# Loading x behind the casting transfers: 180 loads moved from the sync engine's queue to GpSimd's

## The chip, the cores and the metric

The kernel runs on one core of one Trainium2 chip. Its engines work side by side, each through its own list of instructions in order: TensorE (PE, with its weight loads shown apart as PEld), VectorE (DVE), ScalarE (ACT), GpSimd (POOL) and SyncE (SP). Transfers between DRAM and the on-chip memory are issued by SP, ACT or POOL and carried by 16 DMA engines that all of them share. The metric is device time in microseconds from launch to end.

## The reference

Two layers stand one behind the other. The first is an attention through 32 learned rows ("inducing"), for 4 batches of 12480 rows of 128 numbers; the second is a feed-forward layer with a squared ReLU.

```python
B, N, m, C = (4, 12480, 32, 128)
def mab(q, kv):
    s = scale * (q @ kv.transpose(0, 2, 1))
    s = s - s.max(-1, keepdims=True)
    a = np.exp(s)
    a /= a.sum(-1, keepdims=True) + 1e-09
    return a @ kv
h = mab(I, x)                  # 32 rows look at all of x
attn_out = mab(x, h)           # each row of x looks at those 32
hid = np.maximum(attn_out @ w_in, 0.0)      # 128 -> 2048
out = hid * hid @ w_out                     # 2048 -> 128
```

So x is read twice: all of a batch is needed to make h, and then every row again to be looked up in h. All data is float32.

## The kernel before, in words

A batch is cut into 13 units of 960 rows, so that there are 52 units. For each unit there is a *first* pass (scores of x against the 32 learned rows, a running softmax, a running sum h) and later a *second* pass (scores of x against h, softmax, then the feed-forward layer on the result). The first passes of batch 0 are done alone at the start. After that the kernel does the second passes one unit after another, and puts the first passes of the next batch between them: 39 units in all, units 0 to 12 of batches 1 to 3.

**The loads that the change touches.** Each of these 39 first passes needs x in two forms. `xn` is the unit as it lies, one DMA of 120 partitions by 8 rows of 128 numbers (line 418): 960 runs of 512 bytes. `xq` is the unit in blocks, four DMAs of 32 partitions by 30 groups of 32 numbers (line 438): 960 runs of 128 bytes each. DVE turns `xq` into `xt` in one instruction (line 444). There are three `xn` buffers and one `xq` buffer. PE scores `xt` (line 477) and later adds up `xn` under the weights (line 528).

**The feed-forward layer.** A unit is done in two halves of 480 rows, each in four quads j of four 128-wide slices of the hidden layer. For a quad, PE makes the hidden slices (line 895, output h), ACT applies ReLU (line 903) and squares (line 913) into g. To multiply in two parts of lower precision, g is rounded to `hi` and DVE subtracts to get `lo` (line 924). Then PE adds 12 products to the output op (line 940): hi by wo_hi, hi by wo_lo, lo by wo_hi. In quads 0 and 2 DVE does the rounding (line 920). In quads 1 and 3 a DMA on POOL's queue does it, since that queue's transfers can change the type on the way (line 918). These are the *casting transfers*: four per unit, 200 in all, each 128 partitions by 1920 numbers. There are five g, three hi and two lo buffers, counted over all quads.

**Queues.** Before the change SP's queue carries all loads of x, all stores of the output (line 960, four per half unit), and the way of the second pass's weights through DRAM and back (lines 781 and 797). POOL's queue carries, from the first unit's end on, only the casting transfers.

**What sets the order.** The program hands a planner a list of tasks, with an engine, an assumed duration, a due time, the tasks that must come before, and the buffers taken. The planner walks through time with these assumptions and puts each engine's tasks in an order; the instructions are then written in that order, and on the chip each engine goes through its list and waits where it must. POOL's queue is the planner's engine "CAST". So a task moved from one queue to another also changes the order of everything else.

Of the kernel before, what the change touches and what calls it, by code (L numbers as in the profile page):

```python
# [44 lines left out]
class Plan:  # L45
# [36 lines left out]
    def run(self):  # L82
        free = {e: 0.0 for e in self.ENGINES}
        mode = None
        port = moving = 0.0
        taken = {}
        open_ = {e: [] for e in self.ENGINES}
        done = []

        def offer(t):  # L90
            t.ready = 0.0
            for n in t.needs:
                own = n.by in ("PE", "SP") and t.engine == [n.by]
                t.ready = max(t.ready, n.end if own else n.done + self.LATENCY[n.by] + t.late)
            for e in t.engine:
                open_[e].append(t)

        for t in self.tasks:
            t.waiting = len(set(t.needs))
            for n in set(t.needs):  # L100
                n.then.append(t)
        for t in self.tasks:
            if not t.waiting:
                offer(t)

        def room_at(t):
            at = 0.0
            n = {}
            for b in t.takes:
                n[b.tag] = n.get(b.tag, 0) + 1  # L110
                old = taken.get(b.tag, [])
                if b.turn is not None and b.turn != len(old):
                    return None
                i = len(old) + n[b.tag] - 1 - self.room[b.tag]
                if i >= 0:
                    for u in (old[i].users if i < len(old) else ()):
                        if u.end is None:
                            return None
                        at = max(at, u.done + 100.0 + t.late)
            return at  # L120

        while len(done) < len(self.tasks):
            best = None
            for e in self.ENGINES:
                pick = None
                for t in open_[e]:
                    at = room_at(t) if t.takes else 0.0
                    if at is None:
                        continue
                    start = max(free[e], t.ready, at)  # L130
                    if e == "POOL" or (e == "DVE" and t.port):
                        start = max(start, port)
                    key = (0.0 if start <= free[e] + t.near else start, t.due, t.order)
                    if pick is None or key < pick[0]:
                        pick = (key, start, t)
                if pick and (best is None or (pick[1], pick[2].due) < best[0]):
                    best = ((pick[1], pick[2].due), pick[1], pick[2], e)
            if best is None:
                raise RuntimeError("the plan is stuck")
            _, start, t, e = best  # L140
            for k in t.engine:
                open_[k].remove(t)
            ns = t.ns[t.engine.index(e)] if isinstance(t.ns, tuple) else t.ns
            if e == "PE":
                if t.mode != mode:
                    start += self.SWITCH
                mode = t.mode
            t.by, t.start, t.end = e, start, start + ns
            t.done = t.end
            if t.moves:  # L150
                moving = max(moving, t.end + self.FIRST) + t.moves
                t.done = moving + self.LAST + t.lag
            free[e] = t.end
            if e == "POOL" or (e == "DVE" and t.port):
                port = t.end
            for b in t.takes:
                taken.setdefault(b.tag, []).append(b)
            done.append(t)
            for n in t.then:
                n.waiting -= 1  # L160
                if not n.waiting:
                    offer(n)
        return done
# [3 lines left out]
def induced_attention_then_squared_relu_ffn(  # L167
# [8 lines left out]
    nc = tc.nc  # L176
    B, N, C = x.shape
# [4 lines left out]
    NU = N // UNIT  # L182
# [7 lines left out]
    PERIOD, START, T_MAIN, NARROW, STEP = 31000.0, 2500.0, 56000.0, -6000.0, 1300.0  # L190
    W_LOAD = [3000.0, 10500.0, 25400.0, 29700.0, 31000.0, 32000.0, 33000.0, 34000.0]
    W_DUE = [12000.0, 19500.0, 36000.0, 38000.0, 40000.0, 44000.0, 48000.0, 52000.0]
    W_SUM = [50000.0, 54000.0, 57000.0, 60000.0]
    WIDE_NS, STRIPS, AWAY = 870, -34000.0, 0.0
    NEAR, REST_LAG = 450.0, 6000.0
    LAG, CAST_LAG, TWICE, WITHOUT = 1500.0, 1500.0, (3, 6, 9, 14, 27), (12, 25)
# [22 lines left out]
    x_v = x.rearrange("b (u j p) c -> b u p j c", j=NT, p=TS)  # L219
# [31 lines left out]
    add = plan.add  # L251
# [148 lines left out]


    class First:
        def __init__(self, b, u, due, early=False, behind=None, after=None):

            self.b, self.u, self.early, self.n = b, u, early, f"{b}_{u}"
            self.s = s = state.setdefault(b, {"xt": {}, "chain": None, "bxt": {}})
            self.bx = Buffer("early" if early else "xn")
            self.bt = s["bxt"][u] = Buffer("xt")
            lead = 2500 if early else 8000

            def load():
                self.xn = (pools["early"] if early else xn_pool).tile(
                    [TS, NT, C], F32, tag="xn", name=f"xn_{self.n}"
                )
                if early:
                    nc.sync.dma_start(self.xn.rearrange("p (k j) c -> p k (j c)", k=2), xe_v[b, u])
                else:
                    nc.sync.dma_start(self.xn, x_v[b, u])

            loaded = add(  # L420
                "SP", 450, load, due - lead - (4000 if early else 12000), [after],
                takes=[self.bx], late=0, moves=1950 if early else 2300, lag=0.0 if early else LAG,
            )
            self.turned = []
            if not early:
                self.turned.append(self.turn_blocks(due - lead, behind, after))
                return
            for k in range(2):
                self.turned.append(self.turn(k, due - lead + k * lead * 0.4, loaded))

        def turn_blocks(self, due, behind, after):
            bq = Buffer("xq")
            v = {}

            def load():
                v["xq"] = xq_pool.tile([P, 1024], F32, tag="xq", name=f"xq_{self.n}")
                for q in range(Q):
                    nc.sync.dma_start(
                        v["xq"][q * M:(q + 1) * M, :UNIT].rearrange("p (g c) -> p g c", c=M), xq_v[self.b, self.u, q]
                    )  # L440

            def turned():
                self.xt = self.s["xt"][self.u] = xt_pool.tile([C, UNIT], F32, tag="xt", name=f"xt_{self.n}")
                nc.vector.transpose(self.xt, v["xq"][:, :UNIT])  # L444

            t = add("SP", 2200, load, due - 16000, [after], takes=[bq], late=0, moves=3200, lag=LAG)
            return add("DVE", 1070, turned, due, [t, behind], takes=[self.bt], reads=[bq])

        def turn(self, k, due, loaded):
# [423 lines left out]
    def ffn_block(b, u, k, second, t0, opened):  # L873
        n = f"{b}_{u}_{k}"
        s = state[b]
        w = {}
# [3 lines left out]
        sums, done = [], []  # L880

        def quad(j):
# [39 lines left out]
            def low():  # L922
# [1 line left out]
                nc.vector.tensor_sub(v["lo"], v["g"], v["hi"])  # L924

            sq = add("ACT", 1706, square, due + 4000, relus, reads=[bg], late=0)
            cast = j % 2 and 2 < 2 * (b * NU + u) + k < 2 * B * NU - 1
            th = add("CAST" if cast else "DVE", 550 if cast else 1070, high, due + 5700, [sq] + (opened[1:] if j else []), port=not cast,
                     late=200, takes=[bhi], reads=[bg], moves=2800.0 * cast, lag=CAST_LAG * cast)
            tl = add("DVE", 2070, low, due + 7800, [th] + (opened[1:] if j else []), port=True, late=0, takes=[blo], reads=[bg, bhi])  # L930
            for m, (wo, name, from_, buf) in enumerate((
                (wo_hi, "hi", th, bhi), (wo_lo, "hi", th, bhi), (wo_hi, "lo", tl, blo),
# [39 lines left out]

    units = [(b, u) for b in range(B) for u in range(NU)]
    w_ins, w_outs = load_weights(W_DUE)
    firsts = {}
    for u in range(NU):
        firsts[u] = First(0, u, 6000 + START * u, early=True)
        first_alone(firsts[u], 6000 + START * u)
# [15 lines left out]
    open_stage()  # L994
    done = NU - 1

    def next_first(due, after):
        nonlocal done
        if done + 1 == len(units):
            return None  # L1000
        done += 1
        firsts[done] = First(*units[done], due, after=after)
        return firsts[done]

    for w, (b, u) in enumerate(units):
# [10 lines left out]
            seconds[w + 1] = Second(*nxt)  # L1016
        for m in range(1 + (w in TWICE)):
            g = firsts[done] if state.get("last") is not firsts[done] else None
            f = None if w in WITHOUT else next_first(t_u + NARROW, seconds[0].ready[1])
            narrow(None if m or not w else seconds[w + 1], f, g, t_u + NARROW, STEP, before)  # L1020
    for t in plan.run():
        t.fn()
# [31 lines left out]
```

## Time and profile before

| what | value |
|---|---|
| median of 3 runs | 1621.87 us (1618.33 to 1624.77) |
| the profiled execution's own time | 1619.65 us |
| its span, first to last instruction | 1617.9 us |
| granted TensorE clock, mean | 0.997 |
| busy PE, PEld, DVE, ACT, POOL | 99%, 82%, 89%, 95%, 7% |

The span is what the profile shows instruction by instruction; the profiled execution's own time is 1.75 us longer. A busy share is the time in which an engine's instructions ran, waits left out. Matmuls are pipelined, so their records overlap and a busy PE still has to be read through what it waited for. In lists of groups, `out<-in` gives the tiles by the program's names, and what stands behind the bar is the group's busy time, the mean duration of one instruction, the idle time of the engine just before them, and what ended most of that idle time.

### The profile page before, as it was taken

The numbers are of one execution on the slowest core, as the hardware profiler recorded it, in microseconds if no ns is written. First come the engines' busy times: TensorE is split into PE (matmuls) and PEld (weight loads), VectorE is DVE, ScalarE is ACT, GpSimd is POOL, SyncE is SP. The second block draws the span as 40 slices with busy tenths as digits, with TensorE's granted clock in tenths as the row PEclk, the third lists the DMA queues.
The fourth block names the chain that finished last, engine by engine and source line by source line (L and its number), as shares of the span: only waits on it lengthen the run. The fifth ranks groups of instructions, "written<-read, shape, count | busy, mean of one in ns | idle before, by whom it ended". The sixth has DMA issues, their size and how long they took to land.

```text
span 1617.9 us, 23615 instructions
## 1 busy us (share of the span) xinstructions
PE 1594.3 (99%) x8713; PEld 1322.2 (82%) x8713; DVE 1435.6 (89%) x1577; ACT 1541.3 (95%) x1566; POOL 114.8 (7%) x213
## 2 busy tenths in 40 slices
PE   7899999999999999999999999999999999999998
PEld 5488888888888888888888888888888888888886
DVE  4799899988999989998999889989888888989897
ACT  6799999999999999999999999999999999999995
POOL 0000000000000000000000000000000000000000
PEclk9999999999999999999999999999999999999999
DMA  9559889976997797886898898766557555665653
GB/s 225 116 102 225 223 215 217 219 213 182 229 248 201 197 215 205 214 205 189 214 222 232 201 207 207 200 191 177 177 176 222 181 178 178 186 174 183 197 166 89
DMA packets 476735, 315.48 MB, mean 195 GB/s; under 512 B 365996, under 2 KB 445084, under 8 KB 476620
## 3 DMA queue, kind: packets, MB, share of 16 engines
q1 hardware_dynamic: 446508, 116.96, 40.2%
q0 software_dynamic: 29024, 196.84, 34.9%
q8 instruction: 68, 1.11, 0.3%
q14 instruction: 47, 0.39, 0.1%
q10 hardware_dynamic: 1088, 0.18, 0.1%
HBM read 77.15 MB, written 39.67 MB: 72 GB/s over the span
## 4 chain that ended last, share of the span: by engine, by line
PE 90%; DMA 3%; ACT 3%; DVE 2%; issue 1%; SPq 0%; ACTq 0%; DVEq 0%; POOLq 0%
PE op L940 63%; PE h L895 22%; PE na L726 2%; ACT g L903 2%; DMA hi<-g 1%; PE na L477 1%; DMA words_i<-in_moe_w_in_dram 1%; PE nb L528 1%; ACT g L913 1%; DVE lo L924 1%; PE ep L508 1%; DMA xn<-in_x_dram 0%; DMA words_o<-in_moe_w_out_dram 0%; DVE hi L920 0%; PE xtp L459 0%
## 5 line engine op out<-in xcount | busy, mean ns | idle before, releaser
L924 DVE TENSOR_TENSOR lo<-g,hi 128x1920 fp32r<-128x1920 f32 x416 | 882.2, 2144 | 36.0 <-PE op L940 20.7
L903 ACT ACTIVATE g<-h 128x960 f32<-128x960 f32 x832 | 777.8, 983 | 30.3 <-PE h L895 27.6
L913 ACT ACTIVATE g<-g 128x1920 f32<-128x1920 f32 x416 | 759.3, 1825 | 4.3
L895 PE MATMUL h<-st,hw 128*128 128x480 f32 x1664 | 503.4, 385 | 3.5 <-ACT g L903 2.5
L940 PE MATMUL op<-hi,wo_lo 128*128 128x480 f32 x1664 | 475.4, 379 | 0.0
L940 PE MATMUL op<-lo,wo_hi 128*128 128x480 f32 x1664 | 435.2, 381 | 1.3 <-DVE lo L924 1.3
L940 PE MATMUL op<-hi,wo_hi 128*128 128x480 f32 x1664 | 433.1, 380 | 1.8 <-DMA hi<-g 1.8
L895 PEld LDWEIGHTS h<-st,hw 128*128 128x128 f32 x1664 | 304.4, 188 | 64.3 <-ACT g L903 10.1
L940 PEld LDWEIGHTS op<-hi,wo_hi 128*128 128x128 f32 x1664 | 310.9, 188 | 52.5 <-DMA hi<-g 2.8
L940 PEld LDWEIGHTS op<-lo,wo_hi 128*128 128x128 f32 x1664 | 309.5, 188 | 52.4 <-DVE lo L924 2.8
L940 PEld LDWEIGHTS op<-hi,wo_lo 128*128 128x128 f32 x1664 | 311.4, 188 | 50.0 <-issue 1.2
L920 DVE CAST hi<-g 128x1920 fp32r<-128x1920 f32 x216 | 247.6, 1148 | 22.3 <-PE op L940 13.6
L918 POOL DMA_DIRECT2D hi<-g x200 | 110.4, 552 | 1417.5 <-PE op L940 374.9
L956 DVE STREAM_TRANSPOSE rows<-op 128x480 f32<-128x480 f32 x104 | 70.7, 680 | 57.6 <-PE op L940 56.4
L444 DVE STREAM_TRANSPOSE xt<-xq 128x960 f32<-128x960 f32 x39 | 45.4, 1165 | 3.4 <-DMA xq<-in_x_dram 1.9
L726 PEld LDWEIGHTS na<-xt,hT 128*32 128x32 f32 x520 | 19.9, 110 | 24.4 <-issue 17.9
L726 PE MATMUL na<-xt,hT 128*32 128x256 f32 (+2 forms) x520 | 34.8, 351 | 0.4 <-ACT hT L255 0.4
L754 DVE TENSOR_REDUCE z<-d 128x8 f32<-128x256 f32 x52 | 20.7, 398 | 12.7 <-ACT d L750 12.6
L740 DVE STREAM_TRANSPOSE d<-na 128x256 f32<-128x256 f32 x52 | 23.0, 442 | 6.9 <-PE na L726 6.9
L528 PE MATMUL nb<-xn,et 120*32 120x128 f32 x624 | 25.7, 276 | 0.0
L477 PE MATMUL na<-xt,indT 128*32 128x240 f32 x312 | 24.3, 368 | 0.0
L255 ACT COPY xt<-xtp 128x480 f32<-128x480 f32 x26 | 14.2, 559 | 10.6 <-PE xtp L459 10.6
(95 smaller groups left out, 508.0 us busy)
## 6 DMA issues: line engine op xcount, KB each, us to landing
hi<-g POOLq DMA_DIRECT2D x200, 960.0 KB, 4.9
xn<-in_x_dram SPq DMA_DIRECT2D x52, 480.0 KB, 6.4
out_dram<-rows SPq DMA_DIRECT2D x414, 60.0 KB, 3.4
st<-far SPq DMA_DIRECT2D x102, 240.0 KB, 4.6
xq<-in_x_dram SPq DMA_DIRECT2D x156, 120.0 KB, 5.5
far<-sw SPq DMA_DIRECT2D x51, 240.0 KB, 2.5
hw<-hwfar SPq DMA_DIRECT2D x24, 128.0 KB, 4.4
words_i<-in_moe_w_in_dram SPq DMA_DIRECT2D x4, 512.0 KB, 14.9
```

Of the source, the lines that this page charges most:

```text
L444: nc.vector.transpose(self.xt, v["xq"][:, :UNIT])
L477: nc.tensor.matmul(to, indT, from_, start=True, stop=True)
L528: nc.tensor.matmul(where[q * M:(q + 1) * M, :], self.et[:, k, q * M:(q + 1) * M], self.xn[:, 2 * q + k, :], start=(k == 0), stop=(k == 1),)
L726: nc.tensor.matmul(where[q * M:(q + 1) * M, to:to + n], self.s["hT"][:, :2 * M].rearrange("c (m a) -> c m a", a=2)[:, :, 0], self.s["xt"][ ...
L895: nc.tensor.matmul(c["hp"][:, l, :BLK], s["hw", j][:, f % 4 * P:(f % 4 + 1) * P], s["st", u][:, k, :], start=True, stop=True,)
L903: nc.scalar.activation(v["g"][:, 2 * i:2 * i + 2, :], c["hp"][:, :, :BLK], AF.Relu)
L913: nc.scalar.activation(v["g"], v["g"], AF.Square)
L918: nc.gpsimd.dma_start(v["hi"], v["g"])
L920: nc.vector.tensor_copy(v["hi"], v["g"])
L924: nc.vector.tensor_sub(v["lo"], v["g"], v["hi"])
L940: nc.tensor.matmul(w["op"][:, :BLK], wo[:, 4 * j + l, :], v[name][:, l, :], start=len(done) == 1, stop=len(done) == 3 * NF,)
L956: nc.vector.transpose(w["rows"].rearrange("p g c -> p (g c)"), w["op"][:, :BLK])
```

## The change

The loads of x for units 3 and later leave SP's queue and are issued by POOL, each placed behind one chosen casting transfer. `CASTS` says which: for a unit's turn w in the loop, `xq` behind the second half's quad 1 of the unit two before, `xn` behind the same quad of the unit one before; where two first passes fall in one turn, the second pair goes behind other quads. Only units 0 to 2 of batch 1 stay on SP, because no casting transfer is there for them yet; the other 36 of the 39 move. "Behind" is an order in one queue and no wait for the cast to land: `own` makes the planner take the cast's issue, not its landing, as the point from which the load may go. `XN_NS` and 2400 are the planner's assumed issue times.

```diff
-                own = n.by in ("PE", "SP") and t.engine == [n.by]
+                own = n.by in ("PE", "SP", "CAST") and t.engine == [n.by]
...
+    CASTS, XN_NS = (((-2, 1, 1), (-1, 1, 1)), ((-1, 0, 1), (-1, 1, 3))), 900
...
-                    nc.sync.dma_start(self.xn, x_v[b, u])
+                    (nc.gpsimd if casts else nc.sync).dma_start(self.xn, x_v[b, u])
...
             loaded = add(
-                "SP", 450, load, due - lead - (4000 if early else 12000), [after],
+                "CAST" if casts else "SP", XN_NS if casts else 450, load,
+                due - lead - (4000 if early else 12000), [casts[1] if casts else after],
                 takes=[self.bx], late=0, moves=1950 if early else 2300, lag=0.0 if early else LAG,
             )
...
                 for q in range(Q):
-                    nc.sync.dma_start(
+                    (nc.gpsimd if casts else nc.sync).dma_start(
...
-            t = add("SP", 2200, load, due - 16000, [after], takes=[bq], late=0, moves=3200, lag=LAG)
+            t = add(
+                "CAST" if casts else "SP", 2400 if casts else 2200, load, due - 16000, [casts[0] if casts else after],
+                takes=[bq], late=0, moves=3200, lag=LAG,
+            )
...
+            if cast:
+                casts[b * NU + u, k, j] = th
...
+            behind = [casts.get((w + i, k, j)) for i, k, j in CASTS[m]]
+            f = None if w in WITHOUT else next_first(t_u + NARROW, seconds[0].ready[1], all(behind) and behind)
```

What moves is best seen in the lists of instructions. In names such as `hi_5_1_1` the numbers are the unit, the half and the quad (then a running number); `xn_9` and `xq_10` are loads of units 9 and 10 of the next batch.

POOL's list before the change, batch 1, from unit 5's second half to unit 6's:

```order
L918 DMA hi_5_1_1_6563<-g_5_1_1_6500 128x1920
L918 DMA hi_5_1_3_6652<-g_5_1_3_6593 128x1920
L918 DMA hi_6_0_1_6695<-g_6_0_1_6639 128x1920
L918 DMA hi_6_0_3_6788<-g_6_0_3_6699 128x1920
L918 DMA hi_6_1_1_6853<-g_6_1_1_6784 128x1920
```

and the same place in the changed kernel:

```order
L923 DMA hi_5_1_1_6551<-g_5_1_1_6487 128x1920
L419 DMA xn_9_6557<-in_x_dram 120x8x128
L440 DMA xq_10_6568<-in_x_dram 32x30x32 x4
L923 DMA hi_5_1_3_6643<-g_5_1_3_6582 128x1920
L923 DMA hi_6_0_1_6684<-g_6_0_1_6628 128x1920
L923 DMA hi_6_0_3_6777<-g_6_0_3_6690 128x1920
L923 DMA hi_6_1_1_6829<-g_6_1_1_6771 128x1920
```

Five DMAs now stand between the cast of quad 1 and that of quad 3 in the second half; the other three gaps of a unit stay empty. In all 180 DMAs move (36 units by five): POOL's list grows from 218 instructions to 398, SP's shrinks from 829 to 649.

SP's list at this place before:

```order
L418 DMA xn_11_6503<-in_x_dram 120x8x128
L438 DMA xq_11_6568<-in_x_dram 32x30x32 x4
L960 DMA out_dram<-rows_5_0_6619 32x15x32 x4
L781 DMA far_7_6711<-sw_7_6701 256x1x240
L797 DMA st_7_6718<-far_7_6711 64x4x240 x2
L960 DMA out_dram<-rows_5_1_6768 32x15x32 x4
```

and now:

```order
L967 DMA out_dram<-rows_5_0_6608 32x15x32 x4
L786 DMA far_7_6709<-sw_7_6699 256x1x240
L802 DMA st_7_6716<-far_7_6709 64x4x240 x2
L967 DMA out_dram<-rows_5_1_6767 32x15x32 x4
L967 DMA out_dram<-rows_6_0_6896 32x15x32 x4
```

Only the stores and the way through DRAM are left on SP.

DVE's list, where the `xq` loaded above is turned. Before, its load stands ahead of the cast `hi_5_1_1`, and the turn comes after most of unit 6's first half:

```order
L924 TENSOR_TENSOR lo_5_1_3_6723<-g_5_1_3_6593,hi_5_1_3_6652 128x1920
L924 TENSOR_TENSOR lo_6_0_0_6735<-g_6_0_0_6607,hi_6_0_0_6683 128x1920
L956 STREAM_TRANSPOSE rows_5_1_6768<-op_5_1_6581 128x480
L924 TENSOR_TENSOR lo_6_0_1_6770<-g_6_0_1_6639,hi_6_0_1_6695 128x1920
L920 CAST hi_6_0_2_6786<-g_6_0_2_6670 128x1920
...
L740 STREAM_TRANSPOSE d_8_6829<-na_8_6748 128x256
L540 SCALAR_TENSOR_TENSOR hacc_9_6834<-hacc_8_6544,fade_9_6556,nb_9_6758 128x128
L744 TENSOR_REDUCE mx_1_8_6836<-d_8_6829 128x8
L444 STREAM_TRANSPOSE xt_11_6846<-xq_11_6568 128x960
```

and now:

```order
L929 TENSOR_TENSOR lo_5_1_2_6653<-g_5_1_2_6520,hi_5_1_2_6641 128x1920
L769 TENSOR_TENSOR d_7_6528<-d_7_6528,rz_1_7_6651 128x256
L925 CAST hi_6_0_0_6672<-g_6_0_0_6596 128x1920
L773 STREAM_TRANSPOSE a_7_6680<-d_7_6528 128x256
L446 STREAM_TRANSPOSE xt_10_6686<-xq_10_6568 128x960
L777 CAST sw_7_6699<-a_7_6680 128x256
L780 TENSOR_TENSOR sw_7_6699<-a_7_6680,sw_7_6699 128x256
L929 TENSOR_TENSOR lo_5_1_3_6711<-g_5_1_3_6582,hi_5_1_3_6643 128x1920
```

The turn of a unit now stands one cast behind its load and directly ahead of the `lo` that needs the next cast; before it stood several quads later. PE's list holds the same 7795 instructions in both, in another order from about the first moved load on.

More of the change, by code (lines that the diff above doesn't have):

```diff
@@ L402, in induced_attention_then_squared_relu_ffn, with __init__ @@
     class First:
-        def __init__(self, b, u, due, early=False, behind=None, after=None):
+        def __init__(self, b, u, due, early=False, behind=None, after=None, casts=None):
             self.b, self.u, self.early, self.n = b, u, early, f"{b}_{u}"
@@ L425, in __init__ @@
             if not early:
-                self.turned.append(self.turn_blocks(due - lead, behind, after))
+                self.turned.append(self.turn_blocks(due - lead, behind, after, casts))
                 return
@@ L429, in __init__, with turn_blocks @@
                 self.turned.append(self.turn(k, due - lead + k * lead * 0.4, loaded))
-        def turn_blocks(self, due, behind, after):
+        def turn_blocks(self, due, behind, after, casts):
             bq = Buffer("xq")
@@ L926, in quad @@
             sq = add("ACT", 1706, square, due + 4000, relus, reads=[bg], late=0)
-            cast = j % 2 and 2 < 2 * (b * NU + u) + k < 2 * B * NU - 1
+            cast = j % 2 == 1 and 2 < 2 * (b * NU + u) + k < 2 * B * NU - 1
             th = add("CAST" if cast else "DVE", 550 if cast else 1070, high, due + 5700, [sq] + (opened[1:] if j else []), port=not cast,
                      late=200, takes=[bhi], reads=[bg], moves=2800.0 * cast, lag=CAST_LAG * cast)
+            if cast:
+                casts[b * NU + u, k, j] = th
             tl = add("DVE", 2070, low, due + 7800, [th] + (opened[1:] if j else []), port=True, late=0, takes=[blo], reads=[bg, bhi])
@@ L974, in induced_attention_then_squared_relu_ffn @@
     w_ins, w_outs = load_weights(W_DUE)
-    firsts = {}
+    firsts, casts = {}, {}
     for u in range(NU):
@@ L995, in induced_attention_then_squared_relu_ffn, with next_first @@
     done = NU - 1
-    def next_first(due, after):
+    def next_first(due, after, behind):
         nonlocal done
@@ L1001, in next_first @@
         done += 1
-        firsts[done] = First(*units[done], due, after=after)
+        firsts[done] = First(*units[done], due, after=after, casts=behind)
         return firsts[done]
@@ L1018, in induced_attention_then_squared_relu_ffn @@
             g = firsts[done] if state.get("last") is not firsts[done] else None
-            f = None if w in WITHOUT else next_first(t_u + NARROW, seconds[0].ready[1])
+            behind = [casts.get((w + i, k, j)) for i, k, j in CASTS[m]]
+            f = None if w in WITHOUT else next_first(t_u + NARROW, seconds[0].ready[1], all(behind) and behind)
             narrow(None if m or not w else seconds[w + 1], f, g, t_u + NARROW, STEP, before)
```

## The prediction

> **What bounds the kernel now.** I read the table of busy time by stretches first, since it shows where TensorE (PE) stood still. Its columns are the stretch, its length, busy time and count for PE, PEld, DVE, ACT and POOL, then the granted clock, the DMA engines' busy share and GB/s.
>
> ```profile
> 0.00:60.00 60.00, 47.98 (x476) 29.31 (x476) 34.70 (x108) 36.29 (x95) 2.18 (x9) 0.94 0.69 171
> 60.00:100.00 40.00, 37.00 (x192) 26.15 (x191) 35.63 (x46) 37.59 (x47) 2.21 (x5) 1.00 0.80 136
> ...
> 200.00:300.00 100.00, 100.00 (x588) 83.77 (x577) 93.87 (x109) 97.84 (x103) 7.03 (x13) 1.00 0.96 219
> ...
> 800.00:900.00 100.00, 98.59 (x560) 81.55 (x560) 92.29 (x96) 95.39 (x95) 7.37 (x13) 1.00 0.95 220
> 900.00:1000.00 100.00, 99.60 (x542) 83.60 (x541) 91.40 (x105) 96.53 (x100) 8.71 (x14) 1.00 0.91 209
> ...
> 1500.00:1600.00 100.00, 100.00 (x475) 85.63 (x474) 84.89 (x71) 98.90 (x88) 7.00 (x13) 1.00 0.56 172
> 1600.00:1618.00 18.00, 11.54 (x51) 8.81 (x49) 11.59 (x8) 1.84 (x2) 0.00 (x0) 0.92 0.19 27
> sum 1618.00, PE 1594.26 PEld 1322.19 DVE 1435.60 ACT 1541.26 POOL 114.84; mean PE 88.57 PEld 73.46 DVE 79.76 ACT 85.63 POOL 6.38
> ```
>
> PE is idle for 1618.00 - 1594.26 = 23.74 us: 12.02 in the first 60 us, 3.00 from 60 to 100, 6.46 in the last 18, and so only 23.74 - 21.48 = 2.26 us in the 1500 us between. 1.41 of these fall into one stretch, 800 to 900. PE is the bound, and there is almost nothing to take back in the part that the change touches. Next I asked whether "busy" hides slow matmuls: the groups of the two feed-forward lines.
>
> ```profile
> L895 PE MATMUL h<-st,hw 128*128 128x480 f32 x1664 | 503.4, 385 | 3.5 <-ACT g L903 2.5
> L940 PE MATMUL op<-hi,wo_lo 128*128 128x480 f32 x1664 | 475.4, 379 | 0.0
> L940 PE MATMUL op<-hi,wo_hi 128*128 128x480 f32 x1664 | 433.1, 380 | 1.8 <-DMA hi<-g 1.8
> ```
>
> 379 to 385 ns for one shape everywhere, with 1.8 us of idle time ended by a casting transfer, is a stream without holes. It also runs alike at a DMA share of 0.96 and of 0.56 (PE 100.00 in both stretches), so relief of the DMA engines by itself buys PE nothing. Then I asked who waits for casting transfers, in the view of their line, and for `xq`, in the view of that tile; the last row of each is the time from issue to landing.
>
> ```profile
> L918 POOL DMA_DIRECT2D hi<-g x200: 537/537/1235, 119.6 to 1589.7; - x100
> ...
>   DVE lo L924: 13.6, 12
>   PEld op L940: 2.8, 3
>   PE op L940: 1.8, 2
> ...
> DMA to landing us min/median/max: 3.9/4.9/9.1
> ```
>
> ```profile
> L438 SPq DMA_DIRECT2D xq<-in_x_dram x156: 311/620/3146, 62.8 to 1051.0; - x156
> ...
>   DMA xq<-in_x_dram: 1.9, 2
> ...
> DMA to landing us min/median/max: 2.4/5.5/10.0
> ```
>
> Of 200 casts 12 made DVE wait and 2 made PE wait. `xq` made DVE wait twice, for 1.9 us. The largest of these waits, in the order of time:
>
> ```profile
> 808.83 4.23 SPq L438 DMA_DIRECT2D xq<-in_x_dram  x4
> ...
> 809.39 0.54 POOL L918 DMA_DIRECT2D hi<-g  x1 [7.77 <-DVE d L747]
> ...
> 818.50 2.16 DVE L924 TENSOR_TENSOR lo<-g,hi 128x1920 fp32r<-128x1920 f32 x1 [2.68 <-DMA hi<-g]
> ...
> 818.52 1.13 PE L940 MATMUL op<-hi,wo_hi 128*128 128x480 f32 x4 [1.41 <-DMA hi<-g]
> ```
>
> A cast issued at 809.39, right behind four `xq` loads, is the one that took 9.1 us: 818.50 - 809.39. It was 9.1 - 4.9 = 4.2 us later than the median and cost PE 1.41 us. From this I take my price of lateness: some 4.2 - 1.4 = 2.8 us of it are covered, the rest is paid by PE.
>
> **The change part by part.**
>
> *What is removed.* SP loses 36 x 4 `xq` issues of 0.62 us and 36 `xn` issues. None of its remaining transfers is on PE's way (the idle time before L895 names ACT), so this is worth nothing. What can be won is the collision above: loads of x thrown in just ahead of a cast. At the most this is all of PE's wait for casts, 1.8 us.
>
> *What is added on POOL.* It has room: 7.0 us busy in 100. What five more issues cost there the trace does not show for this shape (960 short runs a DMA). The nearest rows are the cast, 128 runs at a median 537 ns (above), and the small copies at the start, 32 runs each:
>
> ```profile
> L789 POOL DMA_DIRECT2D st<-sw x7: 527/533/657, 58.5 to 61.7; - x7
> ```
>
> Four times the runs, and no difference. The low end is then 0.54 us an issue, five in 2.7 us. The high end lets time grow with the runs: 537 x 960 / 128 = 4.03 us, five in 20.1 us. I take 0.8 us, five in 4 us, near the low end since that is what the two rows say. The room for it is the distance to the next cast:
>
> ```profile
> 1233.77 0.54 POOL L918 DMA_DIRECT2D hi<-g  x1 [5.95 <-PE h L895]
> 1241.14 0.54 POOL L918 DMA_DIRECT2D hi<-g  x1 [6.82 <-ACT g L903]
> 1247.66 0.54 POOL L918 DMA_DIRECT2D hi<-g  x1 [5.99 <-ACT g L903]
> 1255.82 0.54 POOL L918 DMA_DIRECT2D hi<-g  x1 [7.62 <-PE op L940]
> ```
>
> 22.05 / 3 = 7.35 us from cast to cast, of which 0.54 are used. 4 us go in without a delay. Queued behind the five issues is the cast of quad 3; behind its landing stands `lo` on DVE, and behind that PE.
>
> *What moves on the DMA engines.* The casts' transfers and the loads now stand in one queue. The shares of the queues:
>
> ```profile
> q1 hardware_dynamic: 446508, 116.96, 40.2%
> q0 software_dynamic: 29024, 196.84, 34.9%
> ```
>
> A cast uses 0.349 x 1617.9 / 200 = 2.8 us of all engines. For `xq` and `xn` I have only landing times. The quickest cast lands in 3.9 us, 1.1 above its 2.8, so at most 2.4 - 1.1 = 1.3 us each for `xq` by its fastest landing. The `xn` group:
>
> ```profile
> L418 SPq DMA_DIRECT2D xn<-in_x_dram x39: 331/564/2905, 66.6 to 1046.9; - x39
> ...
> DMA to landing us min/median/max: 4.3/6.4/18.3
> ```
>
> (its landings are those of the first stage's loads as well) gives 4.3 - 1.1 = 3.2 us. Cast and five loads are then at most 2.8 + 3.2 + 4 x 1.3 = 11.2 us of engine time, against 7.35 to the next cast: up to 3.9 us left in the queue when it comes. At the low end there is nothing left, since the first landings hold fixed time that a queue does not pay five times. I take 1 to 2 us left over, within the 2.8 that are covered.
>
> *What moves on DVE.* The turn of `xq` now stands one cast behind its load, ahead of the next `lo`. Its data must be there about 7.35 + 4.9 = 12.2 us after the first cast's issue. With 11.2 + 1.1 = 12.3 us at the high end it just fails, and with my values it is there some 3 us early. PE's own work does not change.
>
> *The sum*, on the profiled execution's own time: 1619.65 (span 1617.9 and 1.75 around it) - 1.8 = 1617.9 us. The median of the runs shown lies 1621.87 - 1619.65 = 2.2 above that execution, so **1620 us** on its scale. I call this no change; about 0.5%, 8 us, is what a measurement of this kernel can tell from it.
>
> **The rivals.**
>
> *The next cast queues behind the loads (slower).* One mechanism: the casts share a queue with five loads in front of every fourth of them. Before, the two streams came by different queues, and a cast's median landing of 4.9 beside 3.9 at best says that a load costs a cast about 1 us when they meet. If the leftover is the full 3.9 us in every unit, the cast lands 4.9 + 3.9 = 8.8 us after its issue, all but the 9.1 that cost 1.41: 36 x 1.41 = 51 us, 1671 us. In half of the units it is 25 us, **1645 us**. It decides from 2.8 us of leftover. Against it: the planner places DVE and PE for a late landing. The Trainium skill, in "DMA: Bandwidth & Descriptors", section "Queues, rings and completion order", has a rule that speaks for this rival: each DMA engine takes turns between queues at packet granularity, and within a ring it goes in order. By that rule a cast used to get its turns beside x's loads and now gets none until they are through. The late cast at 809.39 shows that taking turns was no full protection either.
>
> *POOL's issue grows with the runs (slower).* At 4.03 us an issue the cast of quad 3 goes out 20.1 + 0.54 - 7.35 = 13.3 us late, 10.5 beyond the cover, in 36 units: 378 us, **about 2000 us**. It decides from (7.35 - 0.54 + 2.8) / 5 = 1.9 us an issue. The 32-run and 128-run rows speak against it.
>
> *DVE's rounding holds POOL up (slower).* DVE's own casts run between these issues:
>
> ```profile
> L920 DVE CAST hi<-g 128x1920 fp32r<-128x1920 f32 x216 | 247.6, 1148 | 22.3 <-PE op L940 13.6
> ```
>
> If each of the five issues had to let one pass, they would take 5 x (0.54 + 1.15) = 8.5 us, and the next cast would go out 1.7 us late. That alone is covered; on top of 3.9 us of leftover it is 5.6 - 2.8 = 2.8 us in 36 units, 101 us, **1721 us**. Against it: a POOL issue takes 537 ns at the minimum and at the median, beside a DVE that is busy 89% of the time. The Trainium skill, "SBUF — State Buffer", section "Who interferes with whom", states the reason: GpSimd writes such transfers' descriptors through a port pair that a VectorE cast can lock for its whole length, and transfers issued from SP are free of it. That rule speaks against moving anything here; no row of this trace shows the lock at work.
>
> *PE gains more than it waited (faster).* 60 to 1600 us hold 3.00 + 2.26 = 5.3 us of idle PE in all. Without any of it the time is 1621.87 - 5.3 = 1617 us, still within 0.5%. Faster, below 1614 us, needs a new order of PE's list that shortens the first 60 us or the last 18 too, by half their 12.02 + 6.46 us: **1612 us**. Nothing in the change reaches there, but the planner's order is new throughout.
>
> **How the numbers follow.** No change 0.67; queueing behind the loads 0.14; long issues 0.08; DVE's rounding 0.04; faster 0.07. So slower has 0.26, faster 0.07, the same 0.67. The range must reach into the first rival: 1612 (all idle time gone and a fast run) to 1655 us (queueing in most units). It leaves out the two expensive rivals, 0.12, the far end of the first and a little below. The forecast's own range is 1613 to 1628.
>
> **What would show it.** Right: POOL's issues of `xq` and `xn` near 0.5 to 1 us, casts landing at a median of 4 to 6 us, PE at 99% and its wait for casts still a few us. Wrong by the first rival: a third group of casts at 8 us and more, always quad 3, with DVE's `lo` idle for "DMA hi<-g" well above 13.6 us. Wrong by the second: POOL's busy time several times 114.84 us. Wrong by the third: issues of uneven length that end with DVE's casts. If DVE waits for `xq` much longer than 1.9 us, it is the turn's place that failed.

## The result, and the profile after

| | before | after |
|---|---|---|
| median of the runs | 1623.32 us (1618.33 to 1625.02, 4 runs) | 1642.41 us (1640.65 to 1642.84, 4 runs) |
| the profiled execution's own time | 1619.65 us | 1642.76 us |
| its span | 1617.9 us | 1641.0 us |

The ratio is 1.0111, with a 95% interval of 1.0092 to 1.013: the change makes the kernel slower by 1.1%, some 18 us. No change was forecast. The time lies inside the range given, but that end of the range was there for another mechanism than the one found.

Of the page of the changed kernel, the totals and five of the groups:

```profile
PE 1603.6 (98%) x8713; PEld 1327.5 (81%) x8713; DVE 1436.7 (88%) x1578; ACT 1545.0 (94%) x1565; POOL 268.1 (16%) x393
...
L947 PE MATMUL op<-hi,wo_hi 128*128 128x480 f32 x1664 | 434.3, 380 | 0.4 <-DMA hi<-g 0.3
...
L923 POOL DMA_DIRECT2D hi<-g x200 | 111.4, 557 | 1279.3 <-PE op L947 368.8
...
L440 POOL DMA_DIRECT2D xq<-in_x_dram x144 | 116.9, 820 | 2.9 <-issue 1.3
...
L533 PE MATMUL nb<-xn,et 120*32 120x128 f32 x624 | 26.9, 285 | 14.2 <-DMA xn<-in_x_dram 14.2
...
L419 POOL DMA_DIRECT2D xn<-in_x_dram x36 | 35.6, 988 | 2.1 <-issue 2.0
```

The row to look at is `nb<-xn,et`, the adding up of `xn` on PE (line 528 before, 533 now). PE stood still 14.2 us in front of it, for the landing of `xn`. No such wait existed before. PE's list of waits says that these are three waits:

```profile
PE nb L533 <- DMA xn<-in_x_dram: 14.2, 3, 5.2
```

The table by stretches says where (same columns as in the prediction):

```profile
100.00:200.00 100.00, 95.21 (x525) 77.84 (x524) 88.69 (x100) 92.45 (x97) 22.29 (x29) 0.97 0.63 158
200.00:300.00 100.00, 95.72 (x536) 80.16 (x535) 86.37 (x99) 92.60 (x96) 24.37 (x32) 0.98 0.84 207
300.00:400.00 100.00, 94.82 (x528) 78.99 (x528) 83.86 (x96) 90.44 (x92) 25.05 (x33) 0.97 0.80 198
400.00:500.00 100.00, 100.00 (x554) 83.10 (x554) 90.16 (x94) 96.24 (x94) 20.53 (x27) 1.00 0.81 219
500.00:1600.00 1100.00, 1099.07 (x5770) 925.24 (x5769) 991.20 (x1025) 1077.56 (x1033) 170.35 (x257) 1.00 0.74 199
```

One wait in each of the three stretches from 100 to 400 us, and each of these stretches also has a granted clock below 1.00. After 400 us nothing is lost any more, although 25 of the 36 moved units are loaded there. Around the first of the three, PE's rows in the order of time:

```profile
150.16 1.03 PE L947 MATMUL op<-lo,wo_hi 128*128 128x480 f32 x4
...
154.07 0.61 PE L482 MATMUL na<-xt,indT 128*32 128x240 f32 x8
159.43 1.11 PE L533 MATMUL nb<-xn,et 120*32 120x128 f32 x16 [4.75 <-DMA xn<-in_x_dram]
160.46 1.17 PE L947 MATMUL op<-hi,wo_hi 128*128 128x480 f32 x2
161.43 1.00 PE L947 MATMUL op<-hi,wo_lo 128*128 128x480 f32 x2
162.23 1.00 PE L900 MATMUL h<-st,hw 128*128 128x480 f32 x2
163.03 1.00 PE L947 MATMUL op<-hi,wo_lo 128*128 128x480 f32 x2
163.83 1.80 PE L947 MATMUL op<-lo,wo_hi 128*128 128x480 f32 x4
165.43 0.65 PE L900 MATMUL h<-st,hw 128*128 128x480 f32 x2
```

and the same place in narrow stretches:

```profile
150.00:154.50 4.50, 4.50 (x28) 3.19 (x26) 2.69 (x8) 4.50 (x9) 3.60 (x5) 1.00 0.99 268
154.50:159.40 4.90, 0.18 (x4) 0.00 (x1) 3.85 (x3) 3.38 (x3) 0.96 (x2) 0.93 1.01 170
159.40:165.50 6.10, 6.07 (x29) 4.89 (x30) 0.35 (x1) 0.97 (x1) 0.89 (x2) 0.50 0.20 28
165.50:172.00 6.50, 6.50 (x32) 5.52 (x31) 6.33 (x7) 5.85 (x9) 0.64 (x1) 1.00 1.02 261
```

PE waits 4.75 us for `xn`. Then it has work again, but the clock granted to it is 0.50 until 165.5: four wide matmuls take 1.80 us there, against 1.03 at 150.16. From 160.46 to 165.43 PE does 12 wide matmuls in 4.97 us; at the pace of the rows ahead of the wait (0.22 us each) that is 2.6 us, so the half clock costs about 2.3 us more. The add-up itself takes 1.03 us to the next row, against 0.59 where the clock is full: another 0.4. This late `xn` therefore costs 4.75 + 2.8, some 7.5 us. Counted in the same way the other two cost 4.28 + 1.6 and 5.18 + 2.5 us: 14.2 us of waiting and 6.9 of half clock, some 21 us for the three, or 7 each.

The wide matmuls of both kernels, counted through and put beside each other by their number, say the same: PE in the changed kernel is 2.7 us behind the kernel before until 151 us, some 10.4 from 169 to 238 us, 14.6 to 16.4 from 258 to 344 us, and 24.0 at 362 us, and from there stays 21 to 25 us behind. The 2.7 us are there before the first moved load goes out (at 123 us), and are not explained by the change. They are also part of why the two profiled executions lie 23 us apart where the medians lie 19.

The page of the Trainium skill on this, "TensorE: Matmul & The Clock Gate", Part 1 "The HAM clock gate", says that the clock is either full or half, and is set back to half after idling for a window of about 3.4 us that runs by itself. On the lengths the trace agrees: in its record of the granted clock the half-clock spells behind the three waits last 6.83, 3.41 and 6.83 us, two, one and two such windows, and in the first 60 us there is one of 3.41 and one of 10.24, three windows. On the idling it does not quite: in a run further down a wait of 2.98 us, shorter than such a window, was followed by half clock too.

**Why `xn` was late.** In five turns of the loop two first passes stand in one turn. In the three of them that fall into batch 1 (units 3, 7 and 11 are the first of each pair) the cast that `xn` was put behind comes just before PE needs it. POOL's list, at unit 3 of batch 1:

```order
L923 DMA hi_2_0_3_1691<-g_2_0_3_1619 128x1920
L923 DMA hi_2_1_1_1751<-g_2_1_1_1695 128x1920
L419 DMA xn_3_1758<-in_x_dram 120x8x128
L440 DMA xq_5_1770<-in_x_dram 32x30x32 x4
L923 DMA hi_2_1_3_1871<-g_2_1_3_1789 128x1920
```

and PE's list:

```order
L947 MATMUL op_2_1_1753<-hi_2_1_0_1731,wo_lo 128x480 x4
L947 MATMUL op_2_0_1646<-hi_2_0_3_1691,wo_hi 128x480 x2
L482 MATMUL na_4_1795<-xt_4_1721,indT 32x240 x4
L533 MATMUL nb_3_1800<-xn_3_1758,et_3_1786 32x128 x8
```

The last part of a name is its running number in the planner's time. The add-up carries 1800, its load 1758: 42 apart. Before the change the same pair stood at 1804 and 1170. The other two are 47 and 46 apart; of all other moved loads the nearest is 97 apart, most near 190 to 200, and none of those made PE wait. In the trace, `xn_3` went out at 151.44 us:

```profile
151.44 0.97 POOL L419 DMA_DIRECT2D xn<-in_x_dram  x1
```

PE was ready for it at about 154.7, 3.2 us later (3.5 and 3.4 us at the other two); the landing of an `xn` takes a median of 7.6 us. In the other two double turns, one each in batches 2 and 3, the loads are 101 and 97 apart and had 8.3 us between issue and add-up, just enough. The other moved loads had 15.8 us or more.

### The profile page after: what moved, and what is told of

Read it like the earlier page. It is cut to its first block, busy times and chain, and to the rows that moved or that the text cites. A ratio compares the mean times of both kernels' runs of the same rounds, so it can differ in the third digit from the quotient of the medians.

```text
span 1641.0 us, 23631 instructions
## 1 busy us (share of the span) xinstructions
PE 1603.6 (98%) x8713; PEld 1327.5 (81%) x8713; DVE 1436.7 (88%) x1578; ACT 1545.0 (94%) x1565; POOL 268.1 (16%) x393
## 4 chain that ended last, share of the span: by engine, by line
PE 83%; DMA 6%; ACT 4%; DVE 4%; issue 3%; SPq 0%; POOL 0%; ACTq 0%; DVEq 0%; POOLq 0%
PE op L947 58%; PE h L900 20%; ACT g L908 2%; DMA hi<-g 2%; DMA xn<-in_x_dram 2%; PE na L731 2%; DVE lo L929 1%; DMA words_i<-in_moe_w_in_dram 1%; PE nb L533 1%; DVE hi L925 1%; ACT g L918 1%; PE na L482 1%; DMA xq<-in_x_dram 1%; PE ep L513 1%; DMA words_o<-in_moe_w_out_dram 0%
## 5 line engine op out<-in xcount | busy, mean ns | idle before, releaser
L929 DVE TENSOR_TENSOR lo<-g,hi 128x1920 fp32r<-128x1920 f32 x416 | 884.4, 2146 | 48.8 <-PE op L947 23.7
L440 POOL DMA_DIRECT2D xq<-in_x_dram x144 | 116.9, 820 | 2.9 <-issue 1.3
L533 PE MATMUL nb<-xn,et 120*32 120x128 f32 x624 | 26.9, 285 | 14.2 <-DMA xn<-in_x_dram 14.2
L533 PEld LDWEIGHTS nb<-xn,et 120*32 120x32 f32 x624 | 19.8, 112 | 20.0 <-issue 15.5
L419 POOL DMA_DIRECT2D xn<-in_x_dram x36 | 35.6, 988 | 2.1 <-issue 2.0
## 6 DMA issues: line engine op xcount, KB each, us to landing
xn<-in_x_dram SPq DMA_DIRECT2D x16, 480.0 KB, 14.6
```

The lines of the kernel that those rows point to most:

```text
L440: (nc.gpsimd if casts else nc.sync).dma_start(v["xq"][q * M:(q + 1) * M, :UNIT].rearrange("p (g c) -> p g c", c=M), xq_v[self.b, self.u, q])
L533: nc.tensor.matmul(where[q * M:(q + 1) * M, :], self.et[:, k, q * M:(q + 1) * M], self.xn[:, 2 * q + k, :], start=(k == 0), stop=(k == 1),)
```

## The experiments

The theory: the whole loss is `xn` coming late at three places, about 7 us each. The rivals: the casts queue behind the loads or POOL's issues are too long (both from the prediction), or the new order as a whole is worse.

**`xn` back to SP's queue, `xq` stays with POOL.**

```diff
-                    (nc.gpsimd if casts else nc.sync).dma_start(self.xn, x_v[b, u])
+                    nc.sync.dma_start(self.xn, x_v[b, u])
...
-                "CAST" if casts else "SP", XN_NS if casts else 450, load,
-                due - lead - (4000 if early else 12000), [casts[1] if casts else after],
+                "SP", 450, load, due - lead - (4000 if early else 12000), [after],
```

> Only xq stays behind the casting transfers on POOL; xn goes back to SP, early, as in the kernel before. Theory (late xn): the 20 us were lost in three places where PE waited for an xn that was issued 3 us before its use (units 3, 7 and 11 of batch 1); without them the time is 1622 us within 4, and PE waits for xn under 1 us after 100 us. Rival (one queue: casts queue behind x's loads, or POOL's longer issues): xq is 144 of the 180 moved DMAs and stays, so at least half of the loss stays, 1632 us or more.

Measured: 1622.99 us (1617.6 to 1635.23), ratio 1.0003, 0.9979 to 1.0028. No wait of PE for `nb` is left in the trace. So moving the 144 `xq` loads, four fifths of the change, costs nothing. It does not yet say whether `xn` is dear because of its queue or because of its place.

**All loads on SP as before; only the three `xn` placed as late as in the change.** The first pairs of turns 3, 6 and 9 get their old queue and the new place; the new lines make the load come after that cast.

```diff
-                "CAST" if casts else "SP", XN_NS if casts else 450, load,
-                due - lead - (4000 if early else 12000), [casts[1] if casts else after],
+                "SP", 450, load, due - lead - (4000 if early else 12000),
+                [add("CAST", 1, lambda: None, due - lead - 12000, [casts[1]]) if casts else after],
...
-            f = None if w in WITHOUT else next_first(t_u + NARROW, seconds[0].ready[1], all(behind) and behind)
+            f = None if w in WITHOUT else next_first(t_u + NARROW, seconds[0].ready[1], w in (3, 6, 9) and not m and behind)
```

> All loads of x on SP as in the kernel before, nothing but casts on POOL; only the xn of turns 3, 6 and 9 is placed as late as in the changed kernel, and the planner is kept from putting its use ahead of its issue. Theory (lateness, whatever the queue): three waits of PE for xn of 5 us or more, each with some us at half clock, 1642 us, between 1636 and 1652. Rival (the loss comes from POOL's queue): 1622 us.

Measured: 1645.35 us (1639.43 to 1647.62), ratio 1.013, 1.0106 to 1.0154. PE's waits in it:

```profile
PE nb L534 <- DMA xn<-in_x_dram: 15.1, 3, 6.2
```

Nothing is on POOL's queue but the casts, and the loss is there in full. It is the place, not the queue. The two runs together clear the queue, the issue times and the other 33 places. Place for place the copy isn't exact: the loads stand 39, 23 and 18 running numbers ahead of their add-ups, and the waits are 5.91, 2.98 and 6.17 us, the second of them shorter than expected.

**All 180 loads on POOL as in the change, but the planner is told that the add-up needs `xn`.** In the program the load was a task that nothing waited for in the planner's list; the add-up's own needs were only the weights.

```diff
-            loaded = add(
+            loaded = self.loaded = add(
...
-            needs += [g.et_done]
+            needs += [g.et_done, g.loaded]
```

> As the changed kernel, all 180 loads on POOL at the same casts, but the planner is told that the adding up of a unit (nb) needs its xn to have landed, so it places nb later. Theory (late xn): 1622 us within 4, with no wait of PE for xn over 1 us. Rival (queue or issue cost): nothing changes there, 1642 us.

Measured: 1620.29 us (1617.57 to 1630.09), ratio 0.9986, 0.9968 to 1.0004. The loads leave where they left in the change. The three add-ups now stand 86, 95 and 102 running numbers behind them, with feed-forward matmuls in between:

```order
L947 MATMUL op_2_1_1753<-hi_2_1_1_1751,wo_lo 128x480 x2
L900 MATMUL h_3_0_2_1828<-st_3_1666,hw_1_850 128x480 x2
L947 MATMUL op_2_1_1753<-lo_2_1_0_1806,wo_hi 128x480 x2
L482 MATMUL na_4_1839<-xt_4_1721,indT 32x240 x4
L533 MATMUL nb_3_1844<-xn_3_1758,et_3_1786 32x128 x8
```

That is the change with its one fault mended, and it ties with the kernel before; a gain is not shown. It is also the forecast of the prediction, met by a kernel that differs from the change in two lines of what the planner is told.

**One and two late loads.** The same, with the planner left unaware for unit 3, or for units 3 and 7, of batch 1.

```diff
-            needs += [g.et_done, g.loaded]
+            needs += [g.et_done, g.n not in ("1_3",) and g.loaded or None]
```

> Edit: the planner knows for 35 of the 36 moved units that PE's add-up needs xn; for unit 3 of batch 1 alone it doesn't, so that one xn is issued 42 running numbers ahead of its add-up, as in the change. Theory (each late xn costs PE its wait of some 5 us and 2 to 3 us of half clock behind it, about 7 us): 1620 + 7 = 1627 us, 1623 to 1631; one PE wait for xn of 4 to 6 us near 154 us, and no other. Rival (the three late loads are only where it shows, and the loss comes from the new order as a whole): 1640 or more, or 1620 with the wait there but taken back later.

> Edit: the same, with units 3 and 7 of batch 1 left out of what the planner knows. Theory: two waits of PE for xn, near 154 and 253 us, 1620 + 14 = 1634 us, 1629 to 1639. Rival (the loss does not go by the number of late loads): the same time as with one, or as with three (1642).

| late loads | median | ratio to before | 95% interval | PE's wait for `xn` |
|---|---|---|---|---|
| 0 (the run above) | 1620.29 us | 0.9986 | 0.9968 to 1.0004 | none |
| 1 | 1628.45 us | 1.0026 | 1.0011 to 1.0041 | 4.5 us |
| 2 | 1633.03 us | 1.0052 | 1.0034 to 1.007 | 9.0 us, 2 |
| 3 (the change) | 1642.41 us | 1.0111 | 1.0092 to 1.013 | 14.2 us, 3 |

In PE's waits with two:

```profile
PE nb L533 <- DMA xn<-in_x_dram: 9.0, 2, 4.5
```

By the ratios (times 1623.5 us) the steps are 6.5, 4.3 and 9.5 us, a mean of 6.8, against about 7 from the trace. The loss goes by the number of late loads. The unevenness of the steps is near what the intervals leave open (0.15% is 2.4 us); in the trace of the change the second place is the cheapest too (5.9 us beside 7.5 and 7.7), by less. The profiled execution with one late load has a second wait that was not expected, 4.0 us for the second pass's weights at 67 us; no moved load has been issued by then, and it does not stand in the run with two.

**`xn` of the other double turns half a unit earlier, one late load left.** An earlier attempt at the same count, this time by moving loads.

```diff
-            behind = [casts.get((w + i, k, j)) for i, k, j in CASTS[m]]
+            places = ((-2, 1, 1), (-1, 0, 1)) if w in TWICE[1:] and not m else CASTS[m]
+            behind = [casts.get((w + i, k, j)) for i, k, j in places]
```

> As the changed kernel, but the xn of the two-pass turns 6, 9, 14 and 27 goes half a unit earlier, behind quad 1 of the first half; only turn 3 keeps its late place. Theory: one of three waits is left, 4 to 5.5 us and some us at half clock behind it, so 1622 + 7 = 1629 us within 3. Rival (queue or issue cost): the same number of loads behind casts, 1642 us.

Measured: 1643.98 us (1635.98 to 1645.81), ratio 1.0118, 1.009 to 1.0145. A miss by 15 us. There is one wait for `xn` as expected, 4.6 us, but DVE now also waits once for the output's stores (5.5 us), and PE for second-pass weights and for the softmax behind DVE. So the edit did not isolate what it was meant to. What of its loss belongs to which of these was not taken apart.

**All `xn` half a unit earlier.**

```diff
-    CASTS, XN_NS = (((-2, 1, 1), (-1, 1, 1)), ((-1, 0, 1), (-1, 1, 3))), 900
+    CASTS, XN_NS = (((-2, 1, 1), (-1, 0, 1)), ((-1, 0, 1), (-1, 0, 3))), 900
```

> Edit: the change as it is, but xn goes behind a cast half a unit earlier (first half in place of second); the planner still doesn't know that the add-up needs it. The shortest distance from an xn to its add-up is then 155 running numbers in place of 42. Theory (lateness of xn is the whole loss, and where POOL issues it matters for nothing else): 1621 us, 1616 to 1627, and no PE wait for xn over 1 us. Rival (five loads behind a cast cost time by themselves, through the queue): 1630 or more.

Measured: 1653.5 us (1644.48 to 1658.96), ratio 1.0157, 1.0128 to 1.0187. No wait for `nb` is left, and yet the run is the slowest of all: a second miss, in the direction of its rival. Its waits, of PE and of DVE:

```profile
PE ep L513 <- ACT e L505: 15.4, 5, 4.8
PE op L947 <- DVE lo L929: 7.6, 5, 5.4
```

```profile
DVE rows L963 <- DMA out_dram<-rows: 27.9, 4, 8.5
...
DVE rows L963 <- issue: 6.6, 1, 6.6
```

DVE's transpose into `rows` (line 963) writes the one buffer that the output's stores read, and four times it had to wait for them. A fifth wait of the same instruction, 6.6 us, is put down to nothing that the profile shows. One of the four, on DVE and then on PE:

```profile
264.62 0.68 DVE L963 STREAM_TRANSPOSE rows<-op 128x480 f32<-128x480 f32 x1 [6.49 <-DMA out_dram<-rows]
265.23 0.37 DVE L492 TENSOR_REDUCE mx<-na 128x1 f32<-128x240 f32 x1
...
265.77 0.15 DVE L498 SCALAR_TENSOR_TENSOR neg<-mx,neg 128x1 f32<-128x1 f32 x1
```

```profile
266.56 0.68 PE L513 MATMUL ep<-ident,e 128*120 128x128 f32 x2 [4.74 <-ACT e L505]
266.89 1.15 PE L900 MATMUL h<-st,hw 128*128 128x480 f32 x2
```

Behind the waiting transpose stands the first pass's maximum, behind that ACT's exponent, behind that PE. The five waits fall into the five double turns, one into each, where POOL's list now has ten loads around two casts, from 136.8 to 153.4 us in the first; the 26 units of the single turns, moved by as much, show none. The stores' landings, of this run, of the change and of the kernel of the next experiment:

```profile
DMA to landing us min/median/max: 1.8/3.5/23.0
```

```profile
DMA to landing us min/median/max: 1.8/4.9/10.6
```

```profile
DMA to landing us min/median/max: 1.8/4.9/12.3
```

So crowding loads does cost time here, as the prediction's first rival had it, but by another way: what reaches PE is not the casts in the same queue (PE's wait for them is 1.3 us in this run) but the stores in the other queue.

**Early and spread: only the first `xn` of a double turn moves, into a gap that held no load.**

```diff
-            behind = [casts.get((w + i, k, j)) for i, k, j in CASTS[m]]
+            places = ((-2, 1, 1), (-2, 1, 3)) if w in TWICE and not m else CASTS[m]
+            behind = [casts.get((w + i, k, j)) for i, k, j in places]
```

> Edit: the change as it is, but in the five turns with two first passes the first pair's xn goes behind a cast three places earlier (quad 3 of the second half two units before), a gap of POOL's list that held no load. Its add-up then comes 250 to 264 running numbers behind the load, the shortest distance of all becomes 94, and the planner is told nothing new. Theory (a late xn costs PE's wait and the half clock behind it; an early one costs nothing as long as its place isn't one where loads are already bunched, which is what made the run with every xn half a unit earlier slow through late stores): 1621 us, 1617 to 1626, no PE wait for xn over 1 us, no wait of DVE for stores, stores landing in at most 13 us. Rival (any shift of xn in these turns costs time, whichever way): 1630 or more.

Measured: 1624.04 us (1619.24 to 1627.75) beside 1624.2 us of the kernel before in the same comparison, ratio 1.0001, 0.9987 to 1.0015. No wait of PE for `nb`, none of DVE for stores. The late loads are mended a second way, with the planner told nothing, and the whole loss is gone again. It also shows that these five `xn` cost nothing by being early. That it was the bunching which made the stores late follows from the contrast of the two; the stores' delay was not produced alone, without moving `xn`.

## Why the prediction was wrong

**What failed is the last sentence of "What moves on DVE": "PE's own work does not change."** The step followed the moved `xq` to the instruction that reads it, and worked out its lead of 12.2 us. It did not do the same for the moved `xn`. The reader of `xn` is PE's add-up, and the lead there is 3.2 to 3.5 us in three of 36 units. The wait for it stood in the sum at nothing, without a reason. The lists of instructions that were read showed units 9 and 10, a single turn, in which the lead is ample. The missing term is three times (wait of 4.7 us + half clock of 2.3 us in the mean) = 21 us; the runs with 0 to 3 late loads put it at 6.8 us each. The half clock, a third of it, had no place in the sum, though it stands in the prediction's table by stretches (0.94 in the first 60 us, where PE idles).

**The other terms, and what was right in them.** In the views of POOL's two lines, of the change:

```profile
L440 POOL DMA_DIRECT2D xq<-in_x_dram x144: 766/768/1785, 123.2 to 1105.8; - x144
...
DMA to landing us min/median/max: 2.7/7.4/10.3
```

```profile
L923 POOL DMA_DIRECT2D hi<-g x200: 528/531/1414, 122.3 to 1612.5; - x100
...
  DVE lo L929: 20.6, 21
  PEld op L947: 1.2, 2
  PE op L947: 0.3, 1
...
DMA to landing us min/median/max: 3.9/4.7/9.8
```

- *What is removed* came true: PE's wait for casts falls from 1.8 to 0.3 us, of 1.8 that could be won.
- *What is added on POOL* came true: 768 ns for an `xq` and, in its view, a median of 963 ns for an `xn`; five in 4 x 0.77 + 0.96 = 4.0 us, the value taken.
- *What moves on the DMA engines* was put too low. The median of all casts, 4.7 us against 4.9 before, mixes two groups. Sorted by what stands ahead of them in POOL's list, the 156 casts with no load ahead land after a median of 4.6 us, and the 28 behind five loads after 7.8 us, 9.8 at most. So some 3 us are left over, where 1 to 2 were taken. DVE's wait for casts rises from 13.6 to 20.6 us, but none of it reaches PE: even 9.8 - 4.6 = 5.2 us were covered, more than the 2.8 taken.
- *What moves on DVE*, for `xq`, was close: its turn waits five times for 4.8 us in all.

**The rivals.** The casts behind the loads did land late, close to the signs that the prediction named for its first rival, but the price was not paid: the kernel whose planner knows of `xn` has the same 28 casts (a median of 8.0 us, 11.3 at most) and 23.7 us of DVE's wait, and ties with the kernel before. That the result lies near the 1645 us of this rival is chance. Long issues are refuted: 0.77 and 0.96 us, where the rival decided from 1.9.

DVE's rounding does hold POOL up, but seldom. The median of an `xq` issue is 768 ns, but of the 180 issues of `xq` and `xn` ten took 1383 to 1903 ns. Each of the ten ran beside a DVE cast of `hi` and ended 0.39 us (`xq`) or 0.46 us (`xn`) behind that cast's end. One of them, and one of the casting transfers in the kernel before (which ends 0.12 us behind DVE's cast):

```profile
264.11 1.90 POOL L419 DMA_DIRECT2D xn<-in_x_dram  x1
...
264.40 1.15 DVE L925 CAST hi<-g 128x1920 fp32r<-128x1920 f32 x1
```

```profile
914.56 1.16 DVE L920 CAST hi<-g 128x1920 fp32r<-128x1920 f32 x1 [0.38 <-issue]
914.60 1.24 POOL L918 DMA_DIRECT2D hi<-g  x1 [5.92 <-PE op L940]
```

The page "SBUF — State Buffer", section "Who interferes with whom", of the Trainium skill would have these issues wait for DVE's casts; these rows agree, and the prediction's "no row of this trace shows the lock at work" overlooked the second of them. In all, the change loses 7.4 us of POOL's time to it in issues of `x`, and POOL is 16% busy; the rival had counted on every issue, 180 in place of ten.

PE's gain beyond what it waited was not seen. (Its 1612 us is 1621.87 - 9.24; with the 5.3 us of the sentence before it would be 1607. Nothing hangs on it.) None of the rivals named the late consumer, so the chance of 0.26 for slower rested on the wrong grounds.

## What to carry to other kernels

When a load is moved later, list every instruction that reads it, each with its distance from the new issue, and look at the shortest distance over all iterations, not at a typical one; three of 36 made the whole loss here. The same holds for a median over mixed groups: that of all casts stayed at 4.7 us while the ones behind five loads went to 7.8, and that of the issues hid the ten that waited. Where something else decides the order (a planner, a scheduler), look whether it knows that the reader needs the load: as long as loads went out early it did not have to, and nothing showed. A wait of a few us on the bounding engine is to be priced with the half clock that comes behind it, here half as much again.

## What the runs showed of the hardware

- In the run with two late loads, waits of PE of 4.53 and 4.51 us were followed by 6.83 and 3.41 us at half clock; a wait of 2.98 us in the run with the three late loads on SP was still followed by 3.41 us. So the price of a wait has a part that its length does not set.
- POOL issues a DMA of 960 runs in 768 ns (128 bytes each) or 963 ns (512 bytes), one of 128 runs in 531 ns: with 7.5 times the runs the time grows by less than a factor of two.
- In the change 16 of POOL's 380 issues ran into a DVE cast from f32 to fp32r and ended a fixed time behind it: 0.12 us with 128 runs, 0.39 or 0.46 us with 960 runs of 128 or 512 bytes. They became 9.7 us longer in all. The 27 others beside which such a cast ran, begun late in the issue or ended early in it, kept about their usual length.
- In the run with all `xn` half a unit earlier, around the five places where ten loads and two casts went out of POOL's queue within 17 us, the casts landed after a median of 8.6 us (13.5 at worst), against 4.7 elsewhere, and the stores on SP's queue after 8.8 us (23.0 at worst), against 3.5. The crowding was paid in both queues; an engine had to wait long only for the stores.
